# Attention and mixer in one planned kernel: a last 1x1 matmul on TensorE behind the last adds, another column of transposed keys that waits for v, and a new table of ranks

## The chip, the cores and the metric

The kernel runs on 1 core of one Trainium2 chip. The metric is the device time of one execution in microseconds (us); the median of several runs counts. TensorE is PE in the profile, VectorE DVE, ScalarE ACT, GpSimd POOL, SyncE SP. PEld is TensorE's weight load. A name such as PEldq or SPq is the queue of that engine's instructions that do no arithmetic: loads of a register, branches, waits, DMA issues.

## The reference

Eight batches of causal attention with a bias from running sums, then an MLP mixer over tokens and over channels. Inputs are float32: q, k, v of shape (8, 8, 576, 64), s of shape (8, 8, 576), and four weight matrices.

```
scores = q @ k^T / sqrt(64)                      # per batch and head, 576 x 576
cum    = cumsum(max(s, 0))
scores = where(causal, -1e9, scores + min(cum_j - cum_i, 0))
x      = (softmax(scores) @ v), heads side by side      # (8, 576, 512)
h      = relu(x^T @ w_tok1) @ w_tok2                    # token mixer, 576 -> 256 -> 576
u      = x + h^T
out    = u + relu(u @ w_ch1) @ w_ch2                    # channel mixer, 512 -> 1536 -> 512
```

## The kernel before

For each batch b (0 to 7) the program goes through these steps.

- q and k are loaded (`qkn`), squared sums are taken for a test on the size of the scores, and both are brought into the form that TensorE needs: early batches by PE transposes against an identity (L882), batches 6 and 7 by DMA transposes on SP (L820). For these each of the two sides i (1, then 0) of `T[i]` is turned in two pieces, columns 0 to 3 (the long transpose, `128x16x128` for batch 7) and column 4 (the short one, `128x4x128`).
- v is loaded (`vf`, L708, on POOL's DMA queue) and merged by DVE with the weights that stand for the bias (`vp`, L726).
- Scores (L956, L947) go to the PSUM tiles `psc` (2 of them), ACT takes the exp (L980, tiles `E`), DVE applies the causal mask (L989, L997), PE multiplies by `vp` (L1043), DVE divides (L1072, L1076) into `x`. Two heads are handled at a time, so there are four such groups, E0 to E3, in a batch.
- The token mixer (L1163, L1233) gives `u`, which is turned by DMA transposes on SP (L1257): `ua` into `uTa` for even batches, `ub` into `uTb` for odd ones; a row of 64 left over is `us`.
- The first channel product (L1298) runs in groups of four matmuls into one of four PSUM tiles `pmx`. ACT or DVE takes the relu out of each (L1305, L1307): `ga` for even batches, `gb` for odd ones; 12 groups for `uTa`, 24 of 320 columns for `uTb`.
- The second channel product goes, for batches 0 to 3, straight to sums and stores (L1329, L1337, L1342). For batches 4 to 7 it is done by seven products on quarters of `g` (L1421; for batch 4 L1548), whose operands are sums and differences of quarters that DVE makes ahead (L1399; for batch 4 L1529), and whose results DVE, POOL and ACT add into the quadrants of the output `of` (L1429, L1431, L1440; for batch 4 L1556, L1558, L1586). Quadrant (n, d) is half n of the rows and half d of the columns, "column half" d. SP stores a quadrant once it has its last add (L1470, for batch 4 L1573). The last product of batch 7 is done in two halves of rows with two PSUM tiles, two adds (L1459) and two stores of 128 x 256 (L1474).

Nothing is left to a scheduler at run time. All steps are put to a planner (`Plan.op`) with their reads, writes, buffers, a rank `prio` and assumed durations on the engines that could do them. `Plan.run` then simulates the engines in program building: of the steps that could start next on an engine, the one with the lowest rank is taken; a buffer is claimed when a step that uses it is placed. The result is one list for each engine, and each engine does its list in order. The ranks are shifted by the table `SHIFT`, eight kinds of steps by eight batches: "quad" to "edge" for the attention and the token mixer, "chan" for L1298, "last", "sum" for the sums of quarters, "out" for the second channel product.

One step serves the order alone. For batch 7, `landed` (L810) is a one-element copy on POOL that reads all of v and is declared as a write of columns of `T[1]`, so that DMA transposes into these columns wait until v has landed.

At the end of the body each engine loads `flagi` into a register (L1745, `TENSOR_LOAD flagi`) and branches on it (L1748): a zero means that the fast form held, and the branch passes by the general form of the computation. DVE has made the flag by 272.2 us, when SP loads it; an engine comes to the load after the last instruction of its own list.

The page gives line numbers of this kernel. In the changed one, lines from about L1465 on are 2 higher (L1529 becomes L1531, L1556 becomes L1558, L1470 becomes L1472), lines from about L1714 on 6 higher (L1745 becomes L1751).

Of the kernel before, what the change touches and what calls it, by code (L numbers as in the profile page):

```python
# [15 lines left out]
PACED = (16, 70)  # L16
TURN = ((0, 4), (4, 5))
SHIFT = {
    "quad": (-91.5, -557, 17.25, -640.25, -242.5, -1211, -1153, 170.25),
    "pair": (280.75, -42.75, -96.5, -432.5, -9.25, -88.25, -1120, -480),  # L20
    "tok": (463, -333, -208, -643, -372.5, -148.5, 180.75, -95.25),
    "edge": (-339.5, 19.5, 183.25, -1041.25, 191, 389.75, 146, 61.5),
    "chan": (460.25, 155.5, -394.75, -10, -45.75, -32.5, -480.75, -610.25),
    "last": (-552.25, 297.75, 54.75, -211.5, 125.75, 358, 116, -169.75),
    "sum": (5.75, 223.75, -222, 751.75, 181.5, -0.5, -94.5, 73),
    "out": (808.25, 1218.75, 11, 21, -30, 262.25, 384.35, -81.3),
}
SEVEN = (4, 5, 6, 7)
INPLACE = (4,)
TP = 3  # L30
# [373 lines left out]
def kernel(  # L404
# [12 lines left out]
    nc = tc.nc  # L417
# [5 lines left out]
    NJ = 5  # L423
# [71 lines left out]
    s_a, s_b = lambda: quarter(3), lambda: quarter(4)  # L495
    t4_sb = sb("t4", [128, QW], BF16, fast)
    t_w = [None, quarter(0), quarter(1), quarter(2), t4_sb[:, :].rearrange("p (c n) -> p c n", c=NCC // 2)]
# [12 lines left out]
    of_all = sb("of", [128, 4, DM], FP32, fast)  # L510
    r_o = Ring("of", [of_all[:, i, :] for i in range(4)])
    r_sc = ring("psc", 2, [128, 1024], FP32, psum)
    r_mx = ring("pmx", 4, [128, 512], FP32, psum)

    P = Plan()
    chain = []
# [89 lines left out]
    for ti, src in enumerate((k, q)):  # L606
# [4 lines left out]
        for f in range(2):  # L611
            def cast0(eng, ti=ti, f=f):
# [4 lines left out]
                else:  # L617
# [19 lines left out]
         writes=["neg0"], prio=-6)  # L637
# [156 lines left out]
    def turn_late(b, behind_=()):  # L794
        odd = b % 2
        n = natb[b]
        T = turned[b] = [Buf(r_T[i]) for i in range(2)]
        for i in range(2):
            T[i].want = odd
            if b == LATE + 1:  # L800
                T[i].gate = tuple(done)
        if b == LATE:
            T[0].gate = tuple(qks)
        def pads4():
            nc.vector.memset(T[0].t[:, NJ - 1, :, 64:128], 0.0)
        if not odd:
            P.op({"DVE": (0.25, 0.4, pads4)}, writes=[(T[0], "pad")], prio=1)
        if b == B - 1:
            def landed():
                nc.gpsimd.tensor_copy(out=T[1].t[0:1, 0, 0, 0:1], in_=vbuf[b][0].t[0:1, NJ - 2, 0, 0:1])  # L810
            o = P.op({"POOL": (0.12, 0.2, landed)}, reads=[(vbuf[b][0], c) for c in range(NJ)],
                     writes=[(T[1], c) for c in range(NJ - 1)], prio=-1, after=chain[-1])
            o.late = -9.0
            chain.append(o)
        for i in (1, 0):
            for c0, c1 in TURN:
                w = 128 if c0 < NJ - 1 or odd else S - c0 * 128

                def trd(i=i, c0=c0, c1=c1, w=w):
                    nc.sync.dma_start_transpose(  # L820
                        out=T[i].t[:, c0:c1, :, 0:w].rearrange("p c m n -> p (c m) n"),
                        in_=n.t[0:w, i, c0:c1, :].rearrange("p c n -> p (c n)"))
                o = P.op({"SP": (1.22 * (c1 - c0) * w / 128, 0, trd)}, reads=[(n, i, c) for c in range(c0, c1)],
                         writes=[(T[i], c) for c in range(c0, c1)], prio=1, dma=0.75 * (c1 - c0) * w / 128)
                o.late = 3.0
                for x in behind_:
                    o.deps.add(x)
# [3 lines left out]
            for c0, c1 in TURN:  # L831
                touch(lambda i=i, c0=c0: turned[b][i].t[0:1, c0, 0, 0:1], [(turned[b][i], c0)], 2)

    done, qks = [], []
    xbuf = {}
    bd = Buf(r_mx, False)

# [549 lines left out]
    def seven_out(b, u, us, g, spans):  # L1387
# [46 lines left out]
        def row(n, d):  # L1434
            return [(o[2 * n + j], d) for j in range(2)]
# [15 lines left out]
        def into(i, pm, a, w_, reads, quads, store):  # L1451
# [3 lines left out]
            for (n, d) in quads:  # L1455
                for j in ([0, 1] if split else [None]):
                    if split:
                        dst = lambda n=n, d=d, j=j: o[2 * n + j].t[:, HD * d : HD * d + HD]
                        P.op(dve(HD, lambda dst=dst, j=j: nc.vector.tensor_tensor(  # L1459
                            out=dst(), in0=pms[j].t[:, HD * j : HD * j + HD], in1=dst(), op=ALU.add)),  # L1460
                            reads=[(pms[j], 0), (o[2 * n + j], d)], writes=[(o[2 * n + j], d)], prio=0)
                    else:
                        plus(lambda n=n, d=d: quad_of(n, d), lambda: two(pm), lambda n=n, d=d: quad_of(n, d),
                             [(pm, 0)] + row(n, d), row(n, d), o)
                    if (n, d) not in store:  # L1465
                        continue

                    def st(n=n, d=d, j=j):
# [3 lines left out]
                        else:  # L1472
# [1 line left out]
                            nc.sync.dma_start(out=out[b, r : r + 128, HD * d : HD * d + HD], in_=o[2 * n + j].t[:, HD * d : HD * d + HD])  # L1474
                    P.op({"SP": (0.6, 0, st)}, reads=row(n, d) if j is None else [(o[2 * n + j], d)], holds=o, prio=0,
                         dma=128 * 0.088 / 16 / (1 if j is None else 2))
        into(3, x[3], s_a, t_w[3], [("sa", 0), ("sa", 1), *[("t3", i) for i in range(HK // TP)]], [(1, 0), (1, 1)], [(1, 1)])
        into(4, x[4], gq[0][1], w[1][0], gk(1), [(0, 0)], [(0, 0)])
        into(5, x[5], s_b, w[1][1], [("sb", 0), ("sb", 1)], [(0, 1)], [(0, 1)])
        into(6, x[6], gq[1][1], t_w[4], gk(1) + [*[("t4", i) for i in range(HK // TP)]], [(1, 0)], [(1, 0)])  # L1480
# [227 lines left out]
    def flag():  # L1708
        nc.vector.tensor_reduce(out=flagf[:, :], in_=bf.t[0:1, 0 : 4 + NSQ], op=ALU.add, axis=mybir.AxisListType.X)
        nc.vector.tensor_copy(out=flagi[:, :], in_=flagf[:, :])  # L1710
    P.op({"DVE": (0.4, 0.7, flag)}, reads=[(bf, 0)], writes=["flag"], prio=-99)

    order = P.run()
    rest = [1.2]  # L1714
# [65 lines left out]
```

## Time and profile before

| what | value |
|---|---|
| median of 3 runs | 289.92 us (289.91 to 290.12) |
| the profiled execution | 290.73 us |
| its span, first to last instruction | 289.1 us |
| granted clock of TensorE | 0.999 |
| PE busy | 278.4 us (96%), 2889 matmuls |
| PEld busy | 176.3 us (61%) |
| DVE busy | 220.2 us (76%) |
| ACT busy | 201.8 us (70%) |
| POOL busy | 116.1 us (40%) |
| DMA | 41.81 MB, mean 145 GB/s |

The span is what the profile sees; the time of an execution has some more around it. The busy shares are means over the whole span: in it there are stretches in which an engine is full and others in which it stands, so the stretch of a change counts, not the mean. A wait is listed with the instruction that waited and with what ended it.

### The profile page before, as it was taken

To read this page: it belongs to the slowest core of one execution; us is meant where nothing else is said; L and a number is where in the kernel's file an instruction comes from. 1 tells how busy PE (TensorE), PEld (TensorE's weight loads), DVE (VectorE), ACT (ScalarE), POOL (GpSimd) and SP (SyncE) were. 2 spreads that over 40 slices of the span, in tenths; PEclk is the share of its full clock that TensorE was granted. 3 is DMA by queue.
4 is the path that set the end of the run, shared out by engine and by line. 5 is a ranking of instruction groups with operands and counts; after the bars stand their busy time and mean duration, and the time that the engine had idled before them with its cause. 6 is when DMAs were issued, how large, how long until landed. Compare 5 with 4: busy or idle time off the path is not lost.

```text
span 289.1 us, 7303 instructions
## 1 busy us (share of the span) xinstructions
PE 278.4 (96%) x2889; PEld 176.3 (61%) x2889; DVE 220.2 (76%) x465; ACT 201.8 (70%) x328; POOL 116.1 (40%) x205
## 2 busy tenths in 40 slices
PE   7999999799999999999999999998999999999992
PEld 3568755556755544557754554566867844687681
DVE  5983578799989976882699999887788937771372
ACT  5796985979999988876994447984453558927600
POOL 8744678767700173169302910242002730140041
PEclk9999999999999999999999999999999999999999
DMA  7999999999962469669975999495223499571014
GB/s 215 227 206 206 205 220 198 224 215 184 223 96 57 129 113 214 137 92 162 199 97 124 126 191 137 96 207 102 59 74 75 72 226 209 76 164 36 2 37 151
DMA packets 67845, 41.81 MB, mean 145 GB/s; under 512 B 47232, under 2 KB 62400, under 8 KB 67808
## 3 DMA queue, kind: packets, MB, share of 16 engines
q0 software_dynamic: 34672, 24.39, 55.7%
q1 hardware_dynamic: 33136, 16.93, 25.4%
q8 instruction: 23, 0.38, 0.6%
q14 instruction: 14, 0.11, 0.1%
HBM read 40.91 MB, written 9.44 MB: 174 GB/s over the span
## 4 chain that ended last, share of the span: by engine, by line


## 5 line engine op out<-in xcount | busy, mean ns | idle before, releaser
L1298 PEld LDWEIGHTS <-wc 128*128 128x128 bf16 x624 | 59.5, 98 | 32.7 <-issue 1.5
L980 ACT ACTIVATE E<-psc 128x1024 bf16<-128x1024 f32 x64 | 62.1, 1020 | 23.7 <-PE psc L956 13.4
L1298 PE MATMUL pmx<-uTb,wc 128*128 128x320 bf16 (+2 forms) x384 | 55.6, 299 | 1.3 <-DVE of L1556 1.3
L1305 ACT ACTIVATE gb<-pmx 128x320 bf16<-128x320 f32 (+2 forms) x73 | 31.8, 437 | 21.9 <-PE pmx L1298 16.2
L1298 PE MATMUL pmx<-uTa,wc 128*128 128x512 bf16 (+1 forms) x240 | 44.5, 337 | 0.0
L708 POOL DMA_DIRECT2D vf<-in_v_dram x39 | 33.6, 869 | 3.3 <-issue 2.7
L726 DVE TENSOR_TENSOR vp<-vf,wT 128x512 bf16<-128x512 f32 (+1 forms) x39 | 27.3, 716 | 5.4 <-DMA vf<-in_v_dram 5.2
L1305 ACT ACTIVATE ga<-pmx 128x512 bf16<-128x512 f32 (+1 forms) x43 | 22.3, 524 | 10.4 <-PE pmx L1298 9.7
L1329 PE MATMUL pmx<-wc,gb 128*128 128x512 bf16 x120 | 28.4, 379 | 0.0
L742 ACT ACTIVATE junk<-qkn 128x1152 bf16<-128x1152 bf16 x24 | 28.0, 1165 | 0.4
L905 DVE COPY kq<-pmx 128x576 bf16<-128x576 bf16 x26 | 18.9, 750 | 8.8 <-PE pmx L882 8.4
L1043 PEld LDWEIGHTS <-E 128*128 128x128 bf16 x576 | 21.0, 97 | 5.0 <-issue 0.3
L1329 PE MATMUL pmx<-wc,ga 128*128 128x512 bf16 x96 | 22.7, 379 | 1.0 <-ACT kq L903 1.0
L1076 DVE TENSOR_TENSOR x<-psc,rc 128x640 bf16<-128x640 f32 x28 | 22.9, 822 | 0.6
L989 DVE TENSOR_TENSOR E<-E,keep 128x512 bf16<-128x512 bf16 x56 | 22.6, 414 | 0.3 <-ACT E L980 0.2
L1431 POOL TENSOR_TENSOR of<-neg,ub 128x512 f32<-128x512 f32 x4 | 4.9, 1218 | 39.8 <-DVE x L1076 20.3
L1043 PE MATMUL psc<-vp,E 128*128 128x65 bf16 x522 | 20.3, 193 | 0.1
L1163 PE MATMUL pmx<-x,w 128*128 128x512 bf16 (+2 forms) x108 | 17.2, 301 | 1.0 <-ACT h L1176 0.6
L1329 PEld LDWEIGHTS <-gb 128*128 128x128 bf16 x120 | 10.8, 98 | 11.6
L868 ACT COPY kqn<-qkn 128x1152 bf16<-128x1152 bf16 x13 | 15.0, 1153 | 2.1 <-DMA qkn<-in_q_dram 2.1
L1233 PE MATMUL pmx<-h,w 128*128 128x512 bf16 x64 | 16.0, 380 | 0.0
L956 PEld LDWEIGHTS <-kq 64*128 64x128 bf16 x240 | 9.8, 94 | 9.7 <-issue 8.2
(184 smaller groups left out, 462.8 us busy)
## 6 DMA issues: line engine op xcount, KB each, us to landing
vf<-in_v_dram POOLq DMA_DIRECT2D x32, 256.0 KB, 7.0
out_dram<-of SPq DMA_DIRECT2D x31, 256.0 KB, 4.1
qkn<-in_k_dram POOLq DMA_DIRECT2D x15, 288.0 KB, 6.4
qkn<-in_q_dram POOLq DMA_DIRECT2D x15, 288.0 KB, 7.0
wc<-in_moe_w_ch_dram POOLq DMA_DIRECT2D x8, 384.0 KB, 8.1
qkn<-in_k_dram POOLq DMA_DIRECT2D x9, 128.0 KB, 5.4
qkn<-in_q_dram POOLq DMA_DIRECT2D x9, 128.0 KB, 10.2
vf<-in_v_dram POOLq DMA_DIRECT2D x7, 128.0 KB, 5.5
```

The lines of the kernel that those rows point to most:

```text
L708: nc.gpsimd.dma_start(out=vf.t[p0 : p0 + n, c, :, :], in_=v[b, :, c * 128 : c * 128 + n, :].rearrange("h p d -> p h d"))
L726: eng.tensor_tensor(out=vp.t[p0 : p0 + n, c, :, 0:D], in0=vf.t[p0 : p0 + n, c, :, :], in1=wT[p0 : p0 + n, cw, b * H : b * H + H].unsqueeze ...
L742: nc.scalar.activation(out=junk[:, :].rearrange("p (t n) -> p t n", t=2), in_=i, func=AF.Square, accum_out=sq[:, col : col + 1])
L905: nc.vector.tensor_copy(out=o, in_=i)
L980: nc.scalar.activation(out=E.t[:, :, 512 * pc : 512 * pc + 512], in_=ps.t[:, :].rearrange("p (e n) -> p e n", e=2), func=AF.Exp, scale=0.125)
L989: nc.vector.tensor_tensor(out=o, in0=o, in1=keep[:, :].unsqueeze(1).unsqueeze(1).to_broadcast([128, 2, 2, 128]), op=ALU.mult)
L1043: nc.tensor.matmul(out=o[:, ic, 0:DE], lhsT=E.t[:, hh, d0 : d0 + 128], rhs=vp.t[:, jc, h + hs_ * hh, 0:DE], start=(jc == j_lo), stop=(jc = ...
L1076: nc.vector.tensor_tensor(out=(x.t[:, :, :].rearrange("p c (m e d) -> p m e c d", e=2, d=D)[:, h // 2] if late else x.t[:, :, :].rearrange ...
L1163: nc.tensor.matmul(out=cols(pm.t[:, :], ha, hb), lhsT=w1[:, NJ if odd and c == NJ - 1 else c, t * 128 : t * 128 + 128], rhs=cols(x.t[:, c, ...
L1298: nc.tensor.matmul(out=pm.t[:, 0 : e - a], lhsT=wc1[:, m, cc * 128 : cc * 128 + 128], rhs=uT.t[:, m, a:e], start=(m == 0), stop=(m == NMC ...
L1305: lambda cc=cc, pm=pm, a=a, e=e: nc.scalar.activation(out=g.t[:, cc, a:e], in_=pm.t[:, 0 : e - a], func=AF.Relu),
L1329: nc.tensor.matmul(out=pm.t[:, na:ne], lhsT=g.t[:, cc, c * 128 : c * 128 + 128], rhs=wc2[:, cc, na:ne], start=(cc == 0), stop=(cc == NCC - 1))
```

## The change

There are four edits. First, all 64 numbers of `SHIFT` are other numbers; no step is added or removed by that, but the planner's lists come out in another order from about 121 us on. Second, `landed` is declared as a write of column 4 of `T[1]` instead of columns 0 to 3. Third, product 3 (counted from 0) of batches 5 to 7 adds into quadrant (1, 1) first and then into (1, 0); it was the other way round. Fourth, PE gets one more step with the highest rank of all, (9999, 0): a matmul of one element that reads `of` and is declared to read what the two last adds (L1459) write, collected in `lasts`. Its result is not used.

```diff
@@ the table: four of its eight rows
-    "edge": (-339.5, 19.5, 183.25, -1041.25, 191, 389.75, 146, 61.5),
-    "chan": (460.25, 155.5, -394.75, -10, -45.75, -32.5, -480.75, -610.25),
-    "sum": (5.75, 223.75, -222, 751.75, 181.5, -0.5, -94.5, 73),
-    "out": (808.25, 1218.75, 11, 21, -30, 262.25, 384.35, -81.3),
+    "edge": (488.75, -59.75, 1158.5, -770.75, 291.5, 799.5, 1275, 685),
+    "chan": (1030.25, 572.75, -70.75, 198.75, 885.5, 1045.75, 198, 89.75),
+    "sum": (96, -585.25, -99.5, 944.25, -17.5, 81, -124.75, 280),
+    "out": (1858, 1527, 144.25, 551.25, 1049.5, 1196, 1357.85, 1564.7),
...
             def landed():
-                nc.gpsimd.tensor_copy(out=T[1].t[0:1, 0, 0, 0:1], in_=vbuf[b][0].t[0:1, NJ - 2, 0, 0:1])
+                nc.gpsimd.tensor_copy(out=T[1].t[0:1, NJ - 1, 0, 0:1], in_=vbuf[b][0].t[0:1, NJ - 2, 0, 0:1])
             o = P.op({"POOL": (0.12, 0.2, landed)}, reads=[(vbuf[b][0], c) for c in range(NJ)],
-                     writes=[(T[1], c) for c in range(NJ - 1)], prio=-1, after=chain[-1])
+                     writes=[(T[1], NJ - 1)], prio=-1, after=chain[-1])
...
-    done, qks = [], []
+    done, qks, lasts = [], [], []
...
+                    if split:
+                        lasts.append((o[2 * n + j], d))
...
-        into(3, x[3], s_a, t_w[3], [("sa", 0), ("sa", 1), *[("t3", i) for i in range(HK // TP)]], [(1, 0), (1, 1)], [(1, 1)])
+        into(3, x[3], s_a, t_w[3], [("sa", 0), ("sa", 1), *[("t3", i) for i in range(HK // TP)]], [(1, 1), (1, 0)], [(1, 1)])
...
+    end = Buf(r_mx, False)
+    tail = of_all[:, 3, 0:1]
+    P.op({"PE": (0.2, 0.3, lambda: nc.tensor.matmul(out=end.t[0:1, 0:1], lhsT=tail, rhs=tail, start=True, stop=True))},
+         reads=lasts, writes=[(end, 0)], prio=(9999, 0))
```

What the lists look like at three places. On DVE, at the merges of v for batch 7, with batch 4's products around them (`ga_97` is batch 4's relu output, `gb_98` batch 5's, the numbers are those of buffers); first before:

```order
L1307 TENSOR_SCALAR gb_98<-pmx_105 128x320
L735 CAST vp_82<-wT 128x32
L737 CAST vp_82<-wT 64x8
L1529 TENSOR_TENSOR ga_97<-ga_97 128x3x256 x2
L726 TENSOR_TENSOR vp_82<-vf,wT 128x8x64 x4
L726 TENSOR_TENSOR vp_82<-vf,wT 64x8x64
L1399 TENSOR_TENSOR vf<-gb_98 128x768
L1556 TENSOR_TENSOR of<-pmx_103,ua_91 128x2x256
L1529 TENSOR_TENSOR ga_97<-ga_97 128x3x256 x2
```

and after:

```order
L1152 COPY x_83<-x_83 64x512
L1531 TENSOR_TENSOR ga_97<-ga_97 128x3x256
L726 TENSOR_TENSOR vp_82<-vf,wT 128x8x64 x4
L726 TENSOR_TENSOR vp_82<-vf,wT 64x8x64
L1399 TENSOR_TENSOR vf<-gb_98 128x768 x2
L1399 TENSOR_TENSOR gb_98<-gb_98 128x3x256
L1399 TENSOR_TENSOR vf<-gb_98 128x768
L1558 TENSOR_TENSOR of<-tmp,ua_91 128x2x256
L1399 TENSOR_TENSOR gb_98<-gb_98 128x3x256
L1399 TENSOR_TENSOR vf<-gb_98 128x768
L1531 TENSOR_TENSOR ga_97<-ga_97 128x3x256 x6
L1558 TENSOR_TENSOR of<-pmx_104,ua_91 128x2x256
```

The merges are followed at once by one difference of `gb` and an eviction of a product of batch 4 before; now six sums and differences of `gb`, one addition and six sums of `ga` come between the merges and the first eviction of a product by DVE.

On SP, the transposes of batch 7's keys and queries (`kq<-qkn`; `16x128` is the long one) and the stores of batch 4 (`128x2x256`), as a piece of the difference:

```order
 L1257 DMA_TRANSPOSE uTb_96<-ub_92 128x4x128 x4
-L1257 DMA_TRANSPOSE uTb_96<-us_93 128x4x128
+L820 DMA_TRANSPOSE kq<-qkn 128x16x128
 L820 DMA_TRANSPOSE kq<-qkn 128x4x128
-L820 DMA_TRANSPOSE kq<-qkn 128x16x128 x2
-L1573 DMA out_dram<-of 128x2x256
+L820 DMA_TRANSPOSE kq<-qkn 128x16x128
 L820 DMA_TRANSPOSE kq<-qkn 128x4x128
-L1573 DMA out_dram<-of 128x2x256 x3
+L1575 DMA out_dram<-of 128x2x256 x4
```

The order was short, long, long, one store, short; it is long, short, long, short, and all four stores come behind them. The transpose of `us` has moved ahead of those of `ub`.

On PE, the end of its list, before:

```order
L1421 LDWEIGHTS gb_98
L1421 MATMUL pmx_103<-t_80,gb_98 128x256
L1745 TENSOR_LOAD flagi
L1748 COMPARE_AND_BRANCH
L300 COMPARE_AND_BRANCH
```

and after:

```order
L1421 LDWEIGHTS gb_98
L1421 MATMUL pmx_104<-t_80,gb_98 128x256
L1716 MATMUL pmx_103<-of 1x1
L1751 TENSOR_LOAD flagi
L1754 COMPARE_AND_BRANCH
```

The 1x1 matmul stands between the last product and the load of the flag.

More of the change, by code (lines that the diff above doesn't have):

```diff
@@ L18 @@
 SHIFT = {
-    "quad": (-91.5, -557, 17.25, -640.25, -242.5, -1211, -1153, 170.25),
-    "pair": (280.75, -42.75, -96.5, -432.5, -9.25, -88.25, -1120, -480),
-    "tok": (463, -333, -208, -643, -372.5, -148.5, 180.75, -95.25),
-    "edge": (-339.5, 19.5, 183.25, -1041.25, 191, 389.75, 146, 61.5),
-    "chan": (460.25, 155.5, -394.75, -10, -45.75, -32.5, -480.75, -610.25),
-    "last": (-552.25, 297.75, 54.75, -211.5, 125.75, 358, 116, -169.75),
-    "sum": (5.75, 223.75, -222, 751.75, 181.5, -0.5, -94.5, 73),
-    "out": (808.25, 1218.75, 11, 21, -30, 262.25, 384.35, -81.3),
+    "quad": (123, -985.5, -467.25, -536.25, 137, -903.5, -418.75, 837.75),
+    "pair": (166.75, -556, -55.5, -681.5, -16.25, 196.5, -714.5, -139),
+    "tok": (1032.5, -584, 21.25, -473.75, 62.25, 234.25, 896, 379),
+    "edge": (488.75, -59.75, 1158.5, -770.75, 291.5, 799.5, 1275, 685),
+    "chan": (1030.25, 572.75, -70.75, 198.75, 885.5, 1045.75, 198, 89.75),
+    "last": (-1036.5, 312, 43, 319.5, -284.25, 371.75, 488.5, -1366.25),
+    "sum": (96, -585.25, -99.5, 944.25, -17.5, 81, -124.75, 280),
+    "out": (1858, 1527, 144.25, 551.25, 1049.5, 1196, 1357.85, 1564.7),
 }
```

## The prediction

> **What bounds the kernel now.** I read the page first, then busy time by stretch (columns: window, then per engine the busy time, PE first), then the list of waits.
>
> ```profile
> PE 278.4 (96%) x2889; PEld 176.3 (61%) x2889; DVE 220.2 (76%) x465; ACT 201.8 (70%) x328; POOL 116.1 (40%) x205
> PEclk9999999999999999999999999999999999999999
> ...
> 160.00:190.00 30.00, 30.00 (x263) 15.28 (x262) 28.48 (x55) 21.09 (x31) 10.72 (x17) 1.00 1.25 140
> 190.00:220.00 30.00, 28.69 (x251) 21.46 (x250) 23.65 (x49) 16.98 (x34) 3.23 (x4) 1.00 0.44 104
> 220.00:250.00 30.00, 30.00 (x245) 18.02 (x244) 22.46 (x43) 17.89 (x28) 9.49 (x14) 1.00 0.74 139
> 250.00:282.00 32.00, 32.00 (x260) 24.99 (x259) 16.61 (x28) 14.61 (x32) 8.60 (x8) 1.00 0.31 64
> 282.00:289.10 7.10, 1.67 (x16) 1.25 (x13) 1.73 (x4) 0.00 (x0) 0.77 (x1) 0.95 0.47 154
> ...
> PE pmx L1298 <- DVE of L1556: 1.3, 1, 1.3
> ...
> 121.40 0.44 PE L882 MATMUL pmx<-ident,kqn 64*128 64x64 bf16 x18
> ```
>
> TensorE bounds it, at full clock. The change keeps all its matmuls and adds one of 1x1, so time can come only from places where PE waits. Its order is unchanged up to the products behind the last row shown (121.5 us), so the idle time before that stays. Behind it PE has one gap: 30.00 - 28.69 = 1.31 us in 190 to 220, and the waits name it (PE waits once, 1.3 us, for an eviction at L1556). Then comes the tail, 7.10 - 1.67 = 5.43 us in which PE has nothing left. Two things can move: 1.31 us in the body, 5.43 us at the end.
>
> **The gap.** The timeline (start, length, instruction, idle time before it and what ended it):
>
> ```profile
> 190.47 4.51 PE L1298 MATMUL pmx<-uTb,wc 128*128 128x320 bf16 x32
> 195.66 0.69 DVE L726 TENSOR_TENSOR vp<-vf,wT 128x512 bf16<-128x512 f32 x1 [1.35 <-DMA vf<-in_v_dram]
> 197.29 3.10 DVE L726 TENSOR_TENSOR vp<-vf,wT 128x512 bf16<-128x512 f32 x3 [0.93 <-DMA vf<-in_v_dram]
> 198.11 0.61 POOL L810 CAST kq<-vf 1x1 bf16<-1x1 f32 x1 [6.60 <-DVE vp L726]
> 198.74 1.92 SPq L820 DMA_TRANSPOSE kq<-qkn  x1
> 200.41 0.56 DVE L1399 TENSOR_TENSOR vf<-gb 128x768 bf16<-128x768 bf16 x1
> 200.89 0.68 DVE L1556 TENSOR_TENSOR of<-pmx,ua 128x512 f32<-128x512 f32 x1
> 201.49 1.02 DVE L1529 TENSOR_TENSOR ga<-ga 128x768 bf16<-128x768 bf16 x2
> 201.63 0.70 PE L1298 MATMUL pmx<-uTb,wc 128*128 128x320 bf16 x4 [1.31 <-DVE of L1556]
> 205.03 1.22 SPq L820 DMA_TRANSPOSE kq<-qkn  x1
> ...
> 212.94 0.61 PE L947 MATMUL psc<-kq 64*128 64x256 bf16 x12
> ```
>
> VectorE works its list in order. The merges of v for batch 7 (L726) wait for v's DMAs and run until 197.29 + 3.10 = 200.39; the eviction L1556 of a batch 4 product stands behind them, and PE needs its accumulator.
>
> In the new order 22 of the 24 L1298 groups of batch 5 on uTb stand in one block ahead of the first of batch 4's seven products, and ScalarE evicts all 22. Each matmul there takes 0.138 us from start to start (7.23 / 52 in the row below, less the overlap), a group of four 0.55. The block, begun at about 190.5, ends near 202.6, while v is still merged until 200.4. Nothing that PE needs is queued behind the merges then, so I cost the gap at -1.31. The cover is ScalarE's pace:
>
> ```profile
> 131.13 7.23 PE L1298 MATMUL pmx<-uTb,wc 128*128 128x320 bf16 x52
> 131.88 6.96 ACT L1305 ACTIVATE gb<-pmx 128x320 bf16<-128x320 f32 x13 [0.65 <-PE pmx L1298]
> 137.00:157.00 20.00, 20.00 (x236) 12.15 (x234) 16.73 (x40) 17.21 (x27) 3.10 (x5) 1.00 0.94 154
> ```
>
> 6.96 / 13 = 0.535 us for an eviction against 0.55 for a group: 22 take 11.8 against 12.1. If that cover went (0.05 us more on each), PE would lose about 1 us.
>
> What is late next is VectorE's list behind the merges: six L1399 (0.56 each), one L1556, six L1529 (1.02 / 2 = 0.51 each), then the evictions. Behind the block PE has a product of twelve (1.3 us; the tail's row below shows 1.47 with overlap), two groups (1.1), then products again. So the last gb is evicted near 202.6 + 1.3 + 1.1 + 0.5 = 205.5; the two L1399 that need it end at 206.6, the first L1529 pair at 207.7, where PE wants it after two more products at 205.0 + 2.6 = 207.6; the six end at 209.7 and the next accumulator is free near 210.4, wanted two products and some scores later, near 210.7. I take 0.2 us here, and 0.3 us for the other places where scores and their use now stand about 4 us apart, as at 138 to 144 and 213 to 220 (two exps on ScalarE and VectorE's masks fit with 0.4 to 0.6 us to spare). In 137 to 157, into which batch 3's L1298 groups move, ACT has 17.21 and DVE 16.73 of 20.00 busy already; the evictions that come (0.535) take the place of L1329's that go, so I expect neither engine to pass PE there. All this waiting: at least 0, at most about 2.6 (two gaps like the 1.31 one); I take 0.5, near the low end, since every slack above came out between -0.1 and +0.6. Body: -1.3 + 0.5 = **-0.8**.
>
> **Transposes and v.** The stand-in write of L810 now gates the short transpose of side 1 instead of the long one, and SP's order becomes long, short, long, short without a store between. Behind the waiting one stand a long and a short transpose and four stores. From 198.74 they need 1.22 + 1.92 + 1.22 = 4.4, so 203.1, with 3.4 to land (median below) 206.5; PE reads kq near 207.6 + 2.6 = 210.2 (212.94 in the row above). Slack 3.7 us: cost nothing. The reversed pair of adds in product 3 has as many instructions; it costs nothing, and the store of quadrant (1,1) leaves one L1429, 0.68 us, sooner.
>
> ```profile
> kq<-qkn SPq DMA_TRANSPOSE x4, 3.4
> ```
>
> **The tail.** Rows by source line (duration min/median/max in ns, first and last start), and the timeline of the end:
>
> ```profile
> L1745 POOLq TENSOR_LOAD <-flagi x1: 502/502/502, 280.5 to 280.5; - x1
> L1745 PEldq TENSOR_LOAD <-flagi x1: 488/488/488, 281.8 to 281.8; - x1
> L1745 DVEq TENSOR_LOAD <-flagi x1: 570/570/570, 283.7 to 283.7; - x1
> L1748 PEldq COMPARE_BRANCH  x1: 393/393/393, 282.4 to 282.4; - x1
> L1748 PEldq EVENT_SEMAPHORE  x1: 51/51/51, 283.7 to 283.7; - x1
> L1748 SPq COMPARE_BRANCH  x1: 78/78/78, 286.5 to 286.5; - x1
> L1474 SPq DMA_DIRECT2D out_dram<-of x2: 826/1206/1587, 284.0 to 285.7; - x2
> DMA to landing us min/median/max: 2.4/3.1/3.7
> L1470 SPq DMA_DIRECT2D out_dram<-of x11: 372/372/395, 229.0 to 283.5; - x11
> ...
> 280.49 2.27 POOL L1431 TENSOR_TENSOR of<-tmp,ub 128x512 f32<-128x512 f32 x2 [1.10 <-DVE tmp L1429]
> 282.20 1.47 PE L1421 MATMUL pmx<-t,gb 128*128 128x256 bf16 x12
> 283.40 0.75 DVE L1459 TENSOR_TENSOR of<-pmx,of 128x256 f32<-128x256 f32 x2
> 283.98 2.50 SPq L1474 DMA_DIRECT2D out_dram<-of  x2
> ...
> q8 instruction: 23, 0.38, 0.6%
> ```
>
> The last matmul ends at 283.67, the last add at 284.15, yet the second half store is issued only at 285.66, because the issue of the first takes 1587 ns and that of the second 826; the eleven stores of L1470 take 372 to 395. What is different here: PE has branched at 282.4, with its next instruction at 283.7, and its instruction queue q8 moves packets of 0.38 MB / 23 = 16 KB that take 0.006 x 16 x 289.1 / 23 = 1.2 us each. A block fetched behind the branch, starting when the stores do, would hold one of the 16 DMA engines for about what the first store is too long (1587 - 372 = 1215 ns). [...]
>
> The 1x1 matmul reads what the last two adds write, so PE's load of the flag goes from 281.84 to about 284.2. Branch (0.6 later) and next instruction (1.9 later) come at 284.8 and 286.1, the fetch after the stores' issue. The matmul itself is short (a 64x64 one takes 0.44 / 18 = 0.024 us; whatever it takes lies beside the landing stores), and PE, near 286.1, still ends ahead of SP. Then store 1 is issued from 283.98 to 284.35, store 2 from about 284.42, 1.24 us sooner. Landing 2.4 us later it is through at 286.8, against 285.66 + 2.4 = 288.06: -1.24, or -1.7 if its own 826 falls to 372 as well; with the 3.7 of the first store's landing it would be 288.1, nothing. DVE's branch stays where it is and fetches too, so I take **-1.1** (0 to -1.7).
>
> **Sum.** Profiled execution: span 289.07, time 290.73, 1.66 outside the span. -0.8 - 1.1 = -1.9: span 287.2, and from the median 289.92 (0.81 below the profiled one) **288.0**.
>
> **Rivals.**
> - PE's sequencer runs past the held matmul, loads the flag at 281.8 as before, and the tail gives nothing: 289.92 - 0.8 = 289.1. Against it: POOL's flag load comes at 280.5, as its last awaited input is done (L1431 starts at 280.49), DVE's at 283.7, as PE's last product is; each sequencer stood at its last semaphore. Chance 0.07. [...]
> - PE is held, but the half stores are slow because three others stand just ahead of them, whatever PE fetches: also 289.1, chance 0.15. For it: a single output store right behind transposes was long too:
>
> ```profile
> 153.79 0.94 SPq L1342 DMA_DIRECT2D out_dram<-of  x1
> ```
>
>  Against: 0.94 is not 1.59, and the L1470 stores, close together too, stayed at 372 to 395.
> - Everything in full: -1.31 with no new waits, -1.7 at the tail: 286.9. Chance 0.12.
> - No change: the new waits take 1.3 and the tail gives nothing: 289.9. Chance 0.08.
> - Slower: v comes later. The list on VectorE has 205.5 - (200.4 + 4 x 0.56) = 2.9 us before it waits for gb anyway, less one L1556 (0.68): about 2.2. If v's loads came another 5.2 us late (as long again as VectorE waits for them in this trace), PE would lose 5.2 - 2.2 = 3.0 and with it the gain: 289.92 - 0.8 + 3.0 - 1.1 = 291.0. It decides where it is slower by 0.58, from about 4.7 us on.
>
> ```profile
> DVE vp L726 <- DMA vf<-in_v_dram: 5.2, 6, 1.4
> ```
>
>  Against: the longest of these six waits is 1.4, and v's issues on POOL keep their place. Chance 0.1, with like mishaps.
> - My forecast, 287.3 to 288.7: chance 0.48.
>
> **How the numbers follow.** The likeliest case gives 288.0. The range runs from all in full (286.9) to the body's 1.31 gap replaced by 1.5 of new waits and no tail gain (290.1); about 0.07 lies below, 0.1 above. A measurement of this kernel can tell about 0.2%, 0.58 us: faster is below 289.34. That holds the forecast, everything in full and most of the first two (0.48 + 0.12 + 0.15); same is the rest of those and most of the fourth (0.07 + 0.06); slower the v case and the rest (0.12).
>
> **What would show it.** Right: no PE wait on L1556 (L1558 there); PE busy 30.00 in 160 to 190 and within 0.3 in 190 to 220; PE's flag load near 283.4 (284.2 less the body's 0.8), behind the last add; both half stores issued within 0.4 us each; span near 287.2. The hold alone is wrong if PE's flag load stays ahead of the last add, or if it moves and the first half store still takes over 1 us. The body is wrong if a PE wait over 0.5 us stands between 121 and 280. Waits of DVE for v over 6 us in all would bring the slower case.

## The result, and the profile after

The changed kernel takes 288.46 us (median of 6 runs, 287.22 to 288.85), the kernel before 290.21 us in the same comparison (6 runs, 289.91 to 290.95). The ratio is 0.9929, 95% interval 0.9906 to 0.9952: about 2 us less, against 0.9934 forecast (288.0 over 289.92). The sum came out right by luck: its two terms were both off, one by 0.67 and the other by 0.70 us, and the errors cancel.

The profiled execution of the changed kernel took 288.37 us with a span of 286.7. First the page's line of engines, then two rows of busy time by stretch and what the list of waits has left of VectorE at v and of PE at accumulators:

```profile
PE 275.9 (96%) x2858; PEld 176.3 (61%) x2891; DVE 216.5 (76%) x461; ACT 203.9 (71%) x331; POOL 115.6 (40%) x206
...
190.00:220.00 30.00, 29.79 (x280) 22.36 (x281) 20.13 (x40) 17.99 (x33) 3.71 (x5) 1.00 0.44 101
280.00:286.70 6.70, 1.89 (x18) 1.36 (x15) 1.76 (x4) 0.00 (x0) 0.79 (x1) 0.91 0.51 163
...
DVE vp L726 <- DMA vf<-in_v_dram: 10.9, 6, 5.6
PE pmx L1737 <- DVE zero L550: 1.5, 1, 1.5
```

The matmul count is lower although the 1x1 matmul was added: some records are missing (2858 matmuls beside 2891 weight loads; before, 2889 of each), so PE's busy time reads a little low. What counts is the list of waits: the 1.3 us for an eviction is gone. The longest wait of PE that is left is the one at the very start, and between 121 us and the end of the last product none is over 0.2 us. The timeline at the old gap (start, length, instruction, idle time before it):

```profile
186.62 4.22 POOL L708 DMA_DIRECT2D vf<-in_v_dram  x5 [0.16 <-issue]
189.97 12.12 PE L1298 MATMUL pmx<-uTb,wc 128*128 128x320 bf16 x88
190.72 11.85 ACT L1305 ACTIVATE gb<-pmx 128x320 bf16<-128x320 f32 x22
191.80 0.69 DVE L726 TENSOR_TENSOR vp<-vf,wT 128x512 bf16<-128x512 f32 x1 [5.62 <-DMA vf<-in_v_dram]
195.88 2.11 DVE L726 TENSOR_TENSOR vp<-vf,wT 128x512 bf16<-128x512 f32 x3 [0.65 <-DMA vf<-in_v_dram]
204.06 0.69 DVE L1558 TENSOR_TENSOR of<-tmp,ua 128x512 f32<-128x512 f32 x1 [2.41 <-ACT tmp L1588]
206.06 2.90 DVE L1531 TENSOR_TENSOR ga<-ga 128x768 bf16<-128x768 bf16 x6
206.94 2.78 PE L1550 MATMUL pmx<-vf,ga 128*128 128x256 bf16 x24
```

The block of 22 groups runs without a break for 12.12 us, ScalarE evicts all of it in 11.85, and VectorE merges v beside it. VectorE even waits: 2.41 us before the addition at 204.06.

The span is 289.07 - 286.70 = 2.37 us shorter. To see where, I cut it at two instructions: the end of the last L1298 group before the orders part, and the end of the last product. The first cut is at the end of the L1298 row here, before (121.47 us) and then after (120.97):

```profile
117.85 3.62 PE L1298 MATMUL pmx<-uTa,wc 128*128 128x512 bf16 x16
```

```profile
117.35 3.62 PE L1298 MATMUL pmx<-uTa,wc 128*128 128x512 bf16 x16
280.23 1.47 PE L1421 MATMUL pmx<-t,gb 128*128 128x256 bf16 x12
282.24 0.19 PE L1716 MATMUL pmx<-of 128*1 128x1 f32 x2 [0.53 <-DVE of L1459]
```

| stretch | before | after | difference |
|---|---|---|---|
| start to the end of that group | 121.47 | 120.97 | -0.50 |
| from there to the end of the last product | 162.20 | 160.73 | -1.47 |
| from there to the end of the span (tail) | 5.40 | 5.00 | -0.40 |

The first 0.50 is not the change's: over the fourteen profiles of this study, this stretch lies anywhere from 120.02 to 121.76 us whatever the kernel. The change gave 1.47 + 0.40 = 1.87 us. (The expectations below give the tail after as 4.96 us.)

The tail by source line (ns min/median/max, first and last start in us):

```profile
L1751 DVEq TENSOR_LOAD <-flagi x1: 572/572/572, 281.8 to 281.8; - x1
L1751 PEldq TENSOR_LOAD <-flagi x1: 780/780/780, 282.2 to 282.2; - x1
L1754 PEldq COMPARE_BRANCH  x1: 388/388/388, 283.1 to 283.1; - x1
L1476 SPq DMA_DIRECT2D out_dram<-of x2: 413/432/452, 282.0 to 282.6; - x2
DMA to landing us min/median/max: 2.2/2.7/3.2
```

TensorE's flag load has moved from 1.8 us ahead of the last product's end to 0.5 us behind it. Both half stores are issued in 0.45 and 0.41 us instead of 1.59 and 0.83. But the second lands 3.2 us after its issue begins; in the kernel before it was 2.4.

### The profile page after: what moved, and what is told of

It reads as the page before. It is cut to its first block, busy times and chain, and to the rows that moved or that the text cites. A ratio compares the mean times of both kernels' runs of the same rounds, so it can differ in the third digit from the quotient of the medians.

```text
span 286.7 us, 7280 instructions
## 1 busy us (share of the span) xinstructions
PE 275.9 (96%) x2858; PEld 176.3 (61%) x2891; DVE 216.5 (76%) x461; ACT 203.9 (71%) x331; POOL 115.6 (40%) x206
## 5 line engine op out<-in xcount | busy, mean ns | idle before, releaser
L1298 PEld LDWEIGHTS <-wc 128*128 128x128 bf16 x624 | 59.5, 98 | 32.1
L1298 PE MATMUL pmx<-uTb,wc 128*128 128x320 bf16 (+2 forms) x384 | 54.9, 300 | 0.0
L1298 PE MATMUL pmx<-uTa,wc 128*128 128x512 bf16 (+1 forms) x238 | 44.0, 337 | 0.1
L726 DVE TENSOR_TENSOR vp<-vf,wT 128x512 bf16<-128x512 f32 (+1 forms) x39 | 25.9, 681 | 11.1 <-DMA vf<-in_v_dram 10.9
L1305 ACT ACTIVATE ga<-pmx 128x512 bf16<-128x512 f32 (+1 forms) x46 | 24.2, 528 | 11.0 <-PE pmx L1298 10.3
L989 DVE TENSOR_TENSOR E<-E,keep 128x512 bf16<-128x512 bf16 x56 | 23.7, 432 | 0.1
L1329 PE MATMUL pmx<-wc,ga 128*128 128x512 bf16 x90 | 21.8, 380 | 0.5 <-ACT kq L903 0.3
L905 DVE COPY kq<-pmx 128x576 bf16<-128x576 bf16 x24 | 17.4, 750 | 1.7 <-PE pmx L882 1.2
L1329 PEld LDWEIGHTS <-gb 128*128 128x128 bf16 x120 | 10.7, 98 | 11.8 <-issue 0.4
L1163 PE MATMUL pmx<-x,w 128*128 128x512 bf16 (+2 forms) x103 | 16.0, 297 | 1.4 <-issue 0.6
L956 PE MATMUL psc<-kq 64*128 64x256 bf16 (+2 forms) x240 | 15.4, 250 | 0.4
L522 POOL CAST seen<-uTb 1x1 f32<-1x1 bf16 x10 | 2.1, 213 | 33.9 <-DMA uTb<-ub 32.7
L1233 PE MATMUL pmx<-h,w 128*128 128x512 bf16 x58 | 15.2, 380 | 0.2
## 6 DMA issues: line engine op xcount, KB each, us to landing
qkn<-in_k_dram POOLq DMA_DIRECT2D x15, 288.0 KB, 5.7
qkn<-in_q_dram POOLq DMA_DIRECT2D x15, 288.0 KB, 6.8
```

The costliest lines, as they stand in the source:

```text
L726: eng.tensor_tensor(out=vp.t[p0 : p0 + n, c, :, 0:D], in0=vf.t[p0 : p0 + n, c, :, :], in1=wT[p0 : p0 + n, cw, b * H : b * H + H].unsqueeze ...
L905: nc.vector.tensor_copy(out=o, in_=i)
L956: nc.tensor.matmul(out=ps.t[:, hh * 512 + c0 : hh * 512 + c0 + e - a], lhsT=kT.t[hh * 64 : hh * 64 + 64, j0 : j0 + 128], rhs=qT.t[hh * 64 ...
L989: nc.vector.tensor_tensor(out=o, in0=o, in1=keep[:, :].unsqueeze(1).unsqueeze(1).to_broadcast([128, 2, 2, 128]), op=ALU.mult)
L1298: nc.tensor.matmul(out=pm.t[:, 0 : e - a], lhsT=wc1[:, m, cc * 128 : cc * 128 + 128], rhs=uT.t[:, m, a:e], start=(m == 0), stop=(m == NMC ...
L1305: lambda cc=cc, pm=pm, a=a, e=e: nc.scalar.activation(out=g.t[:, cc, a:e], in_=pm.t[:, 0 : e - a], func=AF.Relu),
```

## The experiments

There are twelve runs; e0 repeats the changed kernel and e11 repeats e3. Two numbers are read from each profile: the stretch from the L1298 group to the last product's end, and the tail behind it. The tail of one version repeats to about 0.1 us. The stretch repeats to 0.01 us in the new order, while in the old order it lies between 162.20 and 162.55 us. Times of whole runs of one kernel spread by 1 to 4 us. In e4 and e5, lines from L727 on are 1 higher than in the changed kernel, in e6 1 higher than before.

**The changed kernel again (e0).**

> The changed kernel once more, as the yardstick of this group. From its first profile: last product ends 4.96 us before the span does (before: 5.40), no wait of PE on a product's eviction, the two half stores issued in 0.45 and 0.41 us, the second landing 3.2 us after its issue begins. Expected again within 0.1 us; time about 0.993 of before.

Stretch 160.73, tail 5.04, half stores 0.45 and 0.41 us; ratio to before 0.9929 (0.9907 to 0.9952). As expected.

**Without the 1x1 matmul (e1).**

```diff
-    P.op({"PE": (0.2, 0.3, lambda: nc.tensor.matmul(out=end.t[0:1, 0:1], lhsT=tail, rhs=tail, start=True, stop=True))},
-         reads=lasts, writes=[(end, 0)], prio=(9999, 0))
```

> The changed kernel without the 1x1 matmul; all else is the same on every engine. Theory (a block of instructions that TensorE fetches behind its branch holds one of the DMA engines while the half stores are issued): TensorE loads the flag about 1.9 us before its last product ends again, the first half store's issue takes about 1.5 us, the second about 0.8, tail 5.4 us, time 0.4 us above the changed kernel. Rival (the stores were slow because others stood just ahead, and something else in the new order spread them): issue stays at 0.45 and 0.41, tail 4.96, no difference in time. Both: no wait of PE on L1558, since the body is the same.

```profile
L1747 PEldq TENSOR_LOAD <-flagi x1: 493/493/493, 279.0 to 279.0; - x1
L1476 SPq DMA_DIRECT2D out_dram<-of x2: 383/914/1444, 281.2 to 282.7; - x2
DMA to landing us min/median/max: 2.4/3.0/3.6
```

TensorE loads the flag 1.83 us ahead of the last product's end again, and the first half store takes 1.44 us to issue. Tail 5.25, 0.21 to 0.25 above the changed kernel's 5.04 and 5.00 (expected 0.4); the second store was issued quickly (0.38) this time. Stretch 160.73. Ratio to before 0.9942 (0.9918 to 0.9965), which the run's own spread does not separate from the changed kernel's. So with the early branch the first store's issue is long (1.44 us against 0.45); crowding is out.

**Before, with the 1x1 matmul alone (e2).**

```diff
+                    if split:
+                        lasts.append((o[2 * n + j], d))
...
+    end = Buf(r_mx, False)
+    tail = of_all[:, 3, 0:1]
+    P.op({"PE": (0.2, 0.3, lambda: nc.tensor.matmul(out=end.t[0:1, 0:1], lhsT=tail, rhs=tail, start=True, stop=True))},
+         reads=lasts, writes=[(end, 0)], prio=(9999, 0))
```

> The kernel before with the 1x1 matmul alone; its order is otherwise that of before on every engine. Theory (fetch): half stores issued in about 0.45 us each, tail 4.96 us instead of 5.40; PE's wait of 1.3 us on L1556 stays; time 0.4 us below before (ratio 0.9985). Rival (crowding of stores, or a sequencer that runs past the held matmul): the first half store still takes about 1.6 us, tail 5.4, ratio 1.000.

```profile
L1476 SPq DMA_DIRECT2D out_dram<-of x2: 407/434/460, 282.9 to 283.4; - x2
PE pmx L1298 <- DVE of L1558: 1.7, 1, 1.7
```

Issue 0.46 and 0.41 us, tail 4.98; PE's wait stays (1.66 us), stretch 162.55. Ratio 0.9982 (0.9955 to 1.0009), the 0.4 us expected but within what can't be told from nothing. The profile decides it, not the time.

**Why the stores then land late: VectorE held too (e3), and once more (e11).** The raw trace shows the packets of the instruction queues; such a packet is called a fetch here. Times in us relative to the end of the last product. The packets are not labelled by engine: the 16 KB one is put down to TensorE because it moves when TensorE's branch moves (from 1.23 ahead of the product's end before to 1.42 behind it in the changed kernel); the 8 KB ones stay without a name in the table. "Issue" is how long the two half stores' issue took:

```
kernel            16 KB packet (TensorE)   8 KB packets              issue         last store packet   tail
before            0.31 for 1.22            2.07, 3.99                1.59, 0.83    3.93                5.40
e1, no hold       0.25 for 1.09            2.08, 3.61                1.44, 0.38    3.76                5.25
changed           2.48 for 1.16            2.30 for 1.00, 2.55       0.45, 0.41    3.63                5.00
e3, VectorE held  2.52 for 1.25            2.60 for 0.69, 2.98       0.46, 0.40    2.42                3.77
```

In the changed kernel all but nine packets of the last store have begun by 2.43; the nine follow one by one, 0.04 us apart, from 3.29, when the 8 KB packet that started at 2.30 is over. So it is in all seven profiles in which TensorE is held and VectorE is not: the nine begin within 0.01 us of the end of an 8 KB packet. They are eight packets of 1 KB and one of 4 bytes, and eight is a sixteenth of the store's 128 rows of 1 KB. I read this as one of the 16 DMA engines that the page counts being held, which no run shows: the trace does not name the DMA engine of a packet. VectorE is the first to branch behind the product (flag load at 0.05 us, branch at 0.70; SyncE branches at 1.32, TensorE at 1.42), so I took the 8 KB packet at 2.30 for one of its own:

```diff
+    P.op({"DVE": (0.2, 0.3, lambda: nc.vector.tensor_copy(out=seen[0:1, 7:8], in_=end.t[0:1, 0:1]))},
+         reads=[(end, 0)], writes=["end"], prio=9999)
```

> The changed kernel with one more step: VectorE copies the one element that the 1x1 matmul makes, as its last work, so that VectorE's load of the flag (0.05 us behind the last product's end in the changed kernel) comes about 0.8 us later, and the block that it fetches too. In the changed kernel three fetches (VectorE, TensorE, SyncE) begin 2.3 to 2.6 us after the last product, and the last packets of the second half store, which should be through at 2.4, come only at 3.6. Theory A (VectorE's fetch is the one in front of these packets): the second half store lands 2.2 us after its issue begins instead of 3.2, tail 4.0 to 4.2 us, time 0.8 to 1.0 us below the changed kernel (ratio to before 0.990). Theory B (SyncE's own fetch or TensorE's does it): landing stays near 3.2, tail 4.9, time unchanged. If the added wait made VectorE the last engine, the tail would be longer than 4.96.

```profile
L1754 PEldq TENSOR_LOAD <-flagi x1: 786/786/786, 282.9 to 282.9; - x1
L1754 DVEq TENSOR_LOAD <-flagi x1: 785/785/785, 283.1 to 283.1; - x1
L1476 SPq DMA_DIRECT2D out_dram<-of x2: 402/429/456, 282.7 to 283.2; - x2
DMA to landing us min/median/max: 1.9/2.1/2.2
```

It came out as theory A expected: landing 1.9 to 2.2 us, tail 3.77 (lower than forecast), the 8 KB packets at 2.60 and 2.98, the last store packet at 2.42. Time 287.25 us, ratio to before 0.9884 (0.9846 to 0.9922), beside 0.9929 for the changed kernel in the same group.

> The changed kernel with VectorE held too (e3) once more, beside e9 on the same chip: stretch 160.73, tail 3.77, ratio to before 0.988 to 0.990.

Stretch 160.73, tail 3.77, ratio 0.9885 (0.9856 to 0.9914). This is the version that beats both kernels: the same stretch as the changed one and a tail 1.2 us shorter, in both of its profiles. By time alone its lead over the changed kernel is not clear of the spread (0.9884, at most 0.9922, beside 0.9929, at least 0.9907); the tail decides it.

**Held twice (e9).**

```diff
+    P.op({"PE": (0.2, 0.3, lambda: nc.tensor.matmul(out=end.t[0:1, 0:1], lhsT=tail, rhs=tail, start=True, stop=True))},
+         reads=["end"], writes=[(end, 0)], prio=(9999, 1))
+    P.op({"DVE": (0.2, 0.3, lambda: nc.vector.tensor_copy(out=seen[0:1, 6:7], in_=end.t[0:1, 0:1]))},
+         reads=[(end, 0)], writes=["end2"], prio=9999)
```

> The kernel with VectorE held too (e3), with a second 1x1 matmul behind VectorE's copy and a second copy behind that: both flag loads come some 0.4 us later still (1.0 and 1.2 us behind the last product instead of 0.53 and 0.77). Theory: the store packets are through 2.4 us behind the last product and no fetch starts before that in e3 already, so nothing more is to be had; SyncE ends last with 0.5 us to spare over VectorE, so little is lost: tail 3.75 to 3.9 (3.77 in e3), time as e3 (ratio to before 0.988). Rival (TensorE's or VectorE's own end, 0.4 us later, now counts): tail 4.1 or more. Other rival (the fetches still slow the store's receipt): tail below 3.7.

```profile
L1476 SPq DMA_DIRECT2D out_dram<-of x2: 413/430/447, 282.0 to 282.5; - x2
DMA to landing us min/median/max: 2.0/2.1/2.2
```

Tail 3.80, landing the same; ratio 0.9899 (0.9857 to 0.9940). In e3 the fetches that come behind the product begin at 2.52 us and later, behind the last store packet at 2.42, and the longer hold brought nothing more (3.80 beside 3.77).

**Before, with both holds (e10).** The edits of e2 and e3 in the kernel before.

> The kernel before with both holds, the 1x1 matmul and VectorE's copy of its result; the order of the body is that of before. If body and tail add up: stretch 162.2 to 162.6 with PE's wait of 1.3 to 1.7 us on the eviction still there, tail 3.77 instead of 5.40, time 1.6 us below before (ratio 0.9944). If the tail's gain hung on the new order: tail 4.9 or more, ratio 0.998.

```profile
PE pmx L1298 <- DVE of L1558: 1.5, 1, 1.5
```

Stretch 162.44 with PE's wait of 1.54, tail 3.77; ratio 0.9932 (0.9909 to 0.9955). Body and tail add up: against before the tail gives 1.63 us, about what the new order gives in the body (1.47 to 1.82).

**VectorE held 2.8 and 6.3 us longer at v (e4, e5).** In the changed kernel v's merges were through at 197.99 us instead of 200.39. Counted from the first cut, that is 1.9 us sooner, so the gap could be gone for that reason alone. The loads of v themselves begin to be issued at 186.62 us, and at 187.28 in the kernel before:

```profile
187.28 4.23 POOL L708 DMA_DIRECT2D vf<-in_v_dram  x5 [0.30 <-issue]
198.68 1.15 POOL L1558 TENSOR_TENSOR of<-tmp,ua 128x512 f32<-128x512 f32 x1
```

From the first cut that is 0.16 us apart. (The 189.9 in the first expectation below is the start of the fourth of the five issues.) About 0.9 of the 1.9 us is v landing sooner (the last wait for it ends at 195.88 instead of 197.29). The other 1.0 is the last merge, which takes 1.68 us in the kernel before, beside the addition on GpSimd shown here, and 0.69 in the changed one, where no such addition stands there; that the one lengthens the other was not isolated.

```diff
+            many = 5 if b == B - 1 and c == NJ - 2 else 1      # e5: 10
-            alts = {"DVE": (*c_dve(512), lambda mul=mul: mul(nc.vector))}
+            alts = {"DVE": (*c_dve(512), lambda mul=mul, many=many: [mul(nc.vector) for _ in range(many)])}
```

> The changed kernel with one of batch 7's merges of v done five times instead of once (same result; 4 x 0.7 = 2.8 us more on VectorE at that place; nothing else moves). In the changed kernel v's loads were also issued 3.3 us earlier than before (186.6 against 189.9) and its merges ended at 198.0 against 200.4, so the gap could be gone for that reason. Theory (the block of 22 groups that ScalarE evicts covers VectorE): VectorE has until about 201.8 before the chain behind the merges is late, 3.8 us; PE shows no wait for an eviction over 0.3 us, and from the end of the L1298 group at about 121 to the end of the last product it is 160.7 to 161.2 us as in the changed kernel. Rival (v came sooner): with VectorE held as long as before and longer, PE waits 1.3 us or more again, 162.0 or more.

```profile
189.92 12.12 PE L1299 MATMUL pmx<-uTb,wc 128*128 128x320 bf16 x88
196.08 4.31 DVE L726 TENSOR_TENSOR vp<-vf,wT 128x512 bf16<-128x512 f32 x6 [0.30 <-DMA vf<-in_v_dram]
204.01 0.69 DVE L1559 TENSOR_TENSOR of<-tmp,ua 128x512 f32<-128x512 f32 x1 [1.43 <-ACT tmp L1589]
```

The merges end at 196.08 + 4.31 = 200.39, the very time of the kernel before (0.6 us later than there from the first cut), and PE does not wait: stretch 160.73, VectorE still idle 1.43 us ahead of the addition. The earlier v is not the cause; the new order with its block is. No run has the block without the rest of the new table. (Ratio 0.9949, 0.9933 to 0.9966.)

> The same with that merge done ten times: 9 x 0.7 = 6.3 us more on VectorE. This is the price of the slow rival of the prediction, a VectorE held long behind v. Theory: 3.8 us of the 6.3 are covered, PE waits 2.5 us (2.0 to 3.0) in front of batch 4's fourth product or an accumulator behind it; 163.2 us for the stretch. If the cover were only the 2.2 us of the prediction, PE would wait 4.1 us.

```profile
196.29 8.65 DVE L726 TENSOR_TENSOR vp<-vf,wT 128x512 bf16<-128x512 f32 x12 [0.24 <-DMA vf<-in_v_dram]
208.72 2.89 DVE L1532 TENSOR_TENSOR ga<-ga 128x768 bf16<-128x768 bf16 x6
209.32 1.62 PE L1551 MATMUL pmx<-vf,ga 128*128 128x256 bf16 x12 [0.33 <-DVE ga L1532]
212.26 1.47 PE L1551 MATMUL pmx<-vf,ga 128*128 128x256 bf16 x12 [0.77 <-DVE of L1559]
```

PE waits, at the two places expected, but less: stretch 162.19, 1.46 us more instead of 2.5 (by the starts of PE's weight loads, 0.73 at each place). The merges end at 204.94, 6.4 us later than in the changed kernel (with 0.58 for the start of the block, 190.55 against 189.97). Of that, 4.3 were gone at the six sums (208.72 against 206.06 + 0.58), and 0.6 more in the room behind them. So the cover, the time by which VectorE may be late before PE waits, was 4.9 us and not 3.8. Ratio 0.9963 (0.9944 to 0.9982).

**Before, with short merges (e6).**

```diff
+                e = 8 if b == B - 1 else D
-                    out=vp.t[p0 : p0 + n, c, :, 0:D], in0=vf.t[p0 : p0 + n, c, :, :],
+                    out=vp.t[p0 : p0 + n, c, :, 0:e], in0=vf.t[p0 : p0 + n, c, :, 0:e],
```

> The kernel before with batch 7's merges cut to 8 of 64 columns of each head (the other columns of v are left unweighted, so the output of batch 7 is another; some 0.5 us less for each of five merges, the waits for v's loads stay). Theory (PE's gap is VectorE's list held by the merges): VectorE is free about 1.5 us sooner, at 198.9 instead of 200.4, the eviction L1556 follows at once, PE's wait of 1.3 to 1.7 us falls under 0.3 and the stretch from the L1298 group to the last product from 162.2 to about 160.9. Rival (PE waits there for something else that ends together, or the next link takes its place): the wait stays over 0.8, or turns up at another line, and the stretch stays over 161.7.

```profile
198.15 1.15 POOL L1559 TENSOR_TENSOR of<-tmp,ua 128x512 f32<-128x512 f32 x1
198.18 1.21 DVE L727 TENSOR_TENSOR vp<-vf,wT 64x64 bf16<-64x64 f32 x1
198.22 1.79 PE L1299 MATMUL pmx<-uTb,wc 128*128 128x320 bf16 x12
199.42 0.56 DVE L1400 TENSOR_TENSOR vf<-gb 128x768 bf16<-128x768 bf16 x1
199.89 0.68 DVE L1557 TENSOR_TENSOR of<-pmx,ua 128x512 f32<-128x512 f32 x1
200.63 0.70 PE L1299 MATMUL pmx<-uTb,wc 128*128 128x320 bf16 x4 [0.62 <-DVE of L1557]
```

Neither expectation was met: the wait is 0.62, between 0.3 and 0.8. VectorE was free at 199.4, not 198.9: the last merge, cut to 64 x 64, still took 1.21 us beside GpSimd's addition. But the eviction started 0.69 us sooner against PE's groups in front of it (199.89 where PE's began at 198.22, against 200.89 and 198.53), and PE's wait fell by the same 1.31 - 0.62 = 0.69. The two other profiles of the old order, e2 and e10, lie on the same line: from the start of PE's groups to the eviction there are 1.67, 2.36, 2.59 and 2.72 us (e6, before, e10, e2), and PE waits 0.62, 1.31, 1.54 and 1.66, always 1.05 or 1.06 less. That is the theory one for one. Stretch 161.51; ratio 0.9987 (0.9964 to 1.0010). The tail here was 5.41 with issues of 0.45 and 1.14: this time the second issue was the long one, with the 16 KB packet at 0.34.

**The other two edits undone (e7, e8).**

```diff
-                nc.gpsimd.tensor_copy(out=T[1].t[0:1, NJ - 1, 0, 0:1], in_=vbuf[b][0].t[0:1, NJ - 2, 0, 0:1])
+                nc.gpsimd.tensor_copy(out=T[1].t[0:1, 0, 0, 0:1], in_=vbuf[b][0].t[0:1, NJ - 2, 0, 0:1])
-                     writes=[(T[1], NJ - 1)], prio=-1, after=chain[-1])
+                     writes=[(T[1], c) for c in range(NJ - 1)], prio=-1, after=chain[-1])
```

> The changed kernel with the stand-in write of L810 put back to columns 0 to 3 of side 1: on SP the four last transposes come short, long, long, short instead of long, short, long, short, and the first two don't wait for v; nothing else moves. Prediction's theory: it costs nothing, since the transposes are through 3.7 us before PE wants them. Stretch 160.7 to 161.2 us, time as the changed kernel (ratio to before 0.993). Rival: the long transpose then runs beside v's loads and makes them late by 2 us or so; by the cover of 3.8 us that would still cost nothing, but if v came over 4 us later, PE would wait for L1558 again. Second rival: PE waits at L947 for the keys.

```profile
197.08 2.10 DVE L726 TENSOR_TENSOR vp<-vf,wT 128x512 bf16<-128x512 f32 x3 [1.09 <-DMA vf<-in_v_dram]
```

Stretch 160.73, no wait of PE; ratio 0.9935 (0.9909 to 0.9962). v is merged by 199.18, 0.9 us later than in the changed kernel once the start of the block is allowed for (0.26); the seven profiles of the new order that keep both the edit and the merges end them within 0.7 us of one another, counted from the first cut, and all of them sooner than this one. So the changed order of the transposes lets v come sooner by that, within a cover of 4.9.

```diff
-... [(1, 1), (1, 0)], [(1, 1)])
+... [(1, 0), (1, 1)], [(1, 1)])
```

> The changed kernel with the order of product 3's two adds put back to (1,0), (1,1). Prediction's theory: it costs nothing; stretch from the L1298 group at 121 us to the end of the last product 160.73 us, tail 4.9 to 5.05, the three stores of L1472 before the end where they are (1.86, 1.27 and 0.15 us ahead of the last product's end). Rival (the earlier store of quadrant (1,1) made room for the half stores): the first of them comes 0.6 us later and the half stores' issue gets longer, tail over 5.2.

Stretch 160.73, tail 5.03, the three stores at 1.86, 1.27 and 0.15 ahead as before; ratio 0.9937 (0.9910 to 0.9964). The edit changes no list: with either order, under the new table, the planner makes the same list for every engine. In batch 7 the add into (1, 0) stands first, and the add into (1, 1) waits for GpSimd's add into that quadrant. So this run is the changed program once more, and the third of the four edits changes nothing in it.

## Why the prediction was right, point by point

- **What bounds it, and the gap.** Right. The 1.31 us went, the block came out at 12.12 us of PE and 11.85 of ScalarE (12.1 and 11.8 forecast), e6 shows that VectorE behind v was the cause, and e4 and e5 that the new order covers it. In the order of before the gap also varies, 1.31, 1.54 and 1.66 in three profiles.
- **New waits of 0.5: the term that failed in the body.** There were none over 0.2 us. I had worked out slacks of -0.1 to +0.6 and turned "tight" into a price; the runs do not measure these slacks one by one, but none of the tight places cost anything. The nine profiles of the new order apart from e5 all have a stretch of 160.73 us, to the hundredth; the three of the old order have 162.20, 162.44 and 162.55. Body -1.47 instead of -0.8. In all four profiles of the old order, e6 with them, the stretch without its gap is 160.89 or 160.90, so the new order saves another 0.16 us that the prediction did not have; where is open.
- **v's place.** I held that v's issues on POOL keep their place, and they do, to 0.16 us from the first cut. Still v's merges ended 1.9 us sooner, which I had not seen. By e4 that gave nothing.
- **Transposes, `landed`, reversed adds.** Costed at nothing, and worth nothing in time (e7, e8), though e7 shows that the transposes made v land 0.9 us sooner. That the store of quadrant (1,1) would leave 0.68 us sooner was wrong: it is the second of the last three, and stands 1.27 us ahead of the last product's end in both kernels, since the add into (1, 0) comes first in both.
- **The tail: right about the hold, the term mis-sized.** TensorE's hold does move its flag load behind the last adds (0.53 us behind the last product), and the issue of the stores falls as forecast (0.45 and 0.41 us). That the fetch belongs to the branch and holds a DMA engine was my estimate; no run ties a packet to an instruction or to a DMA engine. What the runs show in its place: with TensorE held the 16 KB packet starts 2.48 (e3: 2.52) us behind the last product instead of 0.31 (e1: 0.25), and the first store's issue takes 0.45 (0.46) instead of 1.59 (1.44). The step that failed is "landing 2.4 us later": I took the better landing of before, although VectorE's branch stays where it is. The second store was issued 1.14 us sooner (0.85 us behind the last product instead of 1.99) but landed after 3.2, its last nine packets behind the 8 KB one of 2.30. -0.40 instead of -1.1; with VectorE held too, e3 lands after 2.2 and has a tail 1.2 us shorter.
- **The rival of the sequencer running past the held matmul** is refuted: the flag load came at 282.2, with the matmul at 282.24. Crowded stores are refuted by e1 (without the hold the first half store's issue takes 1.44 us again) and e2 (with the hold alone 0.46).
- **The slow rival** priced a late v with 2.2 us of cover; e5 measured 4.9, so a late v by itself was less likely than the 0.1 that it got.

## What to carry to other kernels

An engine that runs ahead into the closing branch does so at a time that nobody planned. Here a 16 KB instruction packet of 1.09 to 1.25 us moved with TensorE's branch; where it ran beside the half stores' issue, in the kernel before and in e1, that of the first took 1.59 and 1.44 us instead of 0.45. In the changed kernel nine packets of the last store came one by one from the end of an 8 KB packet of 1.00 us. Let each engine that branches late do a tiny dependent instruction behind the last store's input, and look at all of them: holding TensorE alone in the kernel before gave a tail of 4.98 us instead of 5.40, both holds together gave 3.77.

Where an in-order engine must wait for a load, give the bottleneck a block of work that another engine can drain alone, as long as the wait; whether it covers is read from the two paces (0.535 against 0.55 us here). And do not price a place as a loss only because it is tight: here places with an estimated slack of -0.1 to +0.6 us cost nothing.

## What the runs showed of the hardware that was not expected

- Where the 16 KB fetch ran beside the issue of the half stores (from 0.31 us in the kernel before, 0.25 in e1, 0.34 in e6), an issue on SyncE was long: that of the first in the kernel before and in e1 (1.59 and 1.44 us instead of 0.45), that of the second in e6 (1.14). In the changed kernel, where the first fetch behind the last product starts at 2.30 us and the issues are over by 1.27, they were short (0.45 and 0.41) and only the landing was long (3.2 us; 2.2 in e3). Why an issue is long beside a fetch, no run shows.
- The 1x1 matmul on float32 stands in the trace as two weight loads of 80 ns and two matmuls of 164 ns, and TensorE's flag load right behind it takes 780 ns, where it took 488 in the kernel before.
- Nearly all of the spread between profiles of the changed order sits in the first 121 us, which end anywhere from 120.02 to 121.76 us; the 161 us behind them repeat to 0.01 us there (to 0.35 in the old order). What makes the spread was not followed up.
- The last merge of v took 1.68 us in the three full profiles of the old order, each time beside an addition of 128 x 512 on GpSimd (1.15 us), and 0.69 in the changed one without such an addition beside it. That GpSimd is the reason was not isolated.
